# A cached-attention decode kernel: two heads to a K or V tile of 32 KB rows, three tiles instead of six, and the last rows of w4 in a tile of their own

## The chip, the cores and the metric

The kernel runs on one core of a Trainium2 chip. A core has TensorE (PE, with its weight loads shown apart as PEld), VectorE (DVE), ScalarE (ACT), GpSimd (POOL) and SyncE (SP), which here only issues transfers. Sixteen DMA engines move data from HBM into the core's SBUF, which has 128 partitions. The metric is the device time of one execution in microseconds. The kernel before takes 216.84 us (median of three runs, 216.29 to 216.96).

## The reference: what is computed

Four sequences (B = 4) each decode one token of width D = 576. The token is normalized, and two branches work on it.

```python
xn = _layernorm(x)
return x + _A_ref(xn, k_cache, v_cache, wq, wo) + _B_ref(xn, w1, w2, w3, w4)
```

The attention branch A has 32 query heads of width 128 on 16 key/value heads (`rep = 2` query heads share one). Only the last W = 2048 positions of the caches of 8192 count.

```python
q = (x @ wq).reshape(B, Sq, 32, Dh)
scores = einsum("bhqd,bhkd->bhqk", q, k[-W:]) * Dh ** -0.5
o = softmax(scores) @ v[-W:]
return o.reshape(B, Sq, 32 * Dh) @ wo
```

The MLP branch B ends in `x1 + gelu(layernorm(x1) @ w3) @ w4` with F = 4608 hidden values. Its first half adds to x a product of shifted pieces of h; as there is one position only, every shift brings in zeros, so x1 is x, and w1 and w2 are not loaded.

All data are bfloat16. K and V of the window are 67.1 MB, wq 4.7, w3 5.3, w4 5.3 and wo 4.7 MB: 87.2 MB in all, each read once.

## The kernel before, in words

**Tiles.** `load_kv` (L100) loads K or V of one key/value head in one DMA of 2 MB. A partition holds 64 consecutive positions of one batch entry, a row of 16,384 bytes: partition p belongs to batch p mod 4 and to the positions from 64 times p div 4 on. A pool of `NKV = 6` such tiles rotates. All transfers but one small one are issued by SP, in program order, and an issue waits until its tile is free.

**Order of the loads.** The list `order` (L515) is K of heads 0, 1, 2, then V of head h and K of head h + 3 in turn. A 1.15 MB piece of wo goes ahead of every fourth V. w3 follows V of head 2, the last 256 rows of w4 follow V of head 13, and the rest of w4 follows V of head 15 in six pieces. `flush_loads` (L523) issues from this list as long as the counter of free tiles allows; the counter grows at the end of each head's turn. wq, w3 and w4 share one buffer one after the other.

**The work of a head.** VectorE transposes a K tile in 32 x 32 blocks of 32-bit words, in two halves (`k_transpose`, L234). TensorE multiplies the result with the zero-padded queries `qz` (`k_scores`, L327): in four steps s, each of four matmuls of 512 columns. A zero-padded query block puts the eight scores rows of step s to rows 8s and on of a block of 32, so that all 128 partitions of one PSUM bank S are filled. `sm_max` masks the columns that belong to other batch entries and takes the row maximum, `sm_maxT` and `sm_neg` spread the maximum over the rows that share it, `sm_exp` (ScalarE) takes the exponential and its row sums, `sm_turn` transposes E into PT (VectorE), and `pv` (L406) multiplies PT with V in 16 matmuls, of which four run on four column groups of 32. `o_scale` divides by the softmax sums and adds the four slices (VectorE), `o_turn` and `o_sum` bring the result into head order. After each fourth head `o_spread`, `o_pick` and `o_proj` multiply by a piece of wo into the accumulator `acc`.

**Sums of the softmax.** The row sums of a head are split into three bfloat16 terms by GpSimd (`split`) and go through the next head's `sm_maxT` matmul; `sm_den` does it in a matmul of its own for the last head.

**Staging.** The order of all instructions is written out by hand (`manual_schedule`). In the turn of head t the K tile of t is transposed and scored, the softmax of t - 1 is done, PV of t - 2, and scaling of t - 3. The MLP's first product (`mlp_g`, in three slices) and its activation lie in the turn of head 7. Behind the loop come the last heads' softmax and PV, the product with the w4 tail, the last `o_proj`, and 68 matmuls with the rest of w4 (`mlp_out`, recorded as L194 like all products into `acc`). Then `acc` is copied and stored.

**The w4 tail.** The 256 last rows of w4 lie as two rows per partition, loaded in three DMAs of 100, 20 and 8 partitions.

Of the kernel before, what the change touches and what calls it, by code (L numbers as in the profile page):

```python
# [16 lines left out]
NKV = 6  # L17
# [5 lines left out]
def kernel(  # L23
# [29 lines left out]
    NJ = B * rep  # L53
    QD = 32
    NQD = P // QD
    NSL = 4
    SC = NC // NSL
    NI = 2
    CW = D // NI
    NW = SC * QD  # L60
# [20 lines left out]
    ptp = ctx.enter_context(tc.tile_pool(name="pt", bufs=2))  # L81
# [3 lines left out]
    ps_s = ctx.enter_context(tc.tile_pool(name="ps_s", bufs=2, space=PSUM))  # L85
    ps_o = ctx.enter_context(tc.tile_pool(name="ps_o", bufs=2, space=PSUM))
# [13 lines left out]
    def load_kv(kind, h):  # L100
        win = k_win if kind == "K" else v_win
        t = kvp.tile([P, NC, Dh], BF16, tag="kv", name=f"{kind.lower()}n")
        nc.sync.dma_start(out=t[:].rearrange("p c d -> p (c d)"),
                          in_=win[:, h].rearrange("b (p c) d -> p b (c d)", c=NC))
        kv_tiles[kind, h] = t
# [30 lines left out]
    SECTIONS = [(0, NFH), (P * NFH, NFH - 2), (F - 2 * P, 2)]  # L136
    SLOT = [0, NFH, NF - 2]
    W4_PIECES = [0, NFH, NFH + 5, NFH + 10, NFH + 14, NFH + 15, NFH + 16]
    TAIL_PARTS = [(0, 100), (100, 120), (120, P)]
    TAIL_AFTER = 13  # L140

    def w4_section(k):
        r0, n = SECTIONS[k]
        return B_w4[r0:r0 + P * n, :].rearrange("(p i) n -> p i n", i=n)

    def load_w4_tail():
        t = wp.tile([P, NF, D], BF16, tag="w", name="w4_sb")
        w_tiles["w4"] = t
        for lo, hi in TAIL_PARTS:
            nc.sync.dma_start(out=t[lo:hi, NF - 2:NF, :], in_=w4_section(2)[lo:hi])  # L150

    def load_w4():
        t = w_tiles["w4"]
        for lo, hi in zip(W4_PIECES, W4_PIECES[1:]):
            k = lo // NFH
            nc.sync.dma_start(out=t[:, lo:hi, :], in_=w4_section(k)[:, lo - SLOT[k]:hi - SLOT[k], :])

# [22 lines left out]
    gT = const.tile([P, NF, B], BF16, name="gT")  # L180
    op = const.tile([P, WOR, B], BF16, name="op")

    accs = [ps_acc.tile([P, CW], F32, name=f"acc{i}") for i in range(2)]
    for acc in accs:
        nc.vector.memset(acc[:], 0.0)

    def acc_of(i):
        return accs[i * 2 // NI][i * QD:i * QD + B, :]

# [44 lines left out]
    def k_transpose(h, half):  # L234
        c0 = half * 2 * SC
        src = kv_tiles["K", h][:].bitcast(I32)[:, c0:c0 + 2 * SC, :].rearrange("p c (ib i) -> p ib c i", i=QD)
        kt = ktp.tile([P, 2, 2 * SC, QD], I32, tag="kt")
        nc.vector.transpose(out=kt[:], in_=src)  # L238
        kts[h, half] = kt
# [3 lines left out]
    for kb in range(NQD):  # L243
# [3 lines left out]
    nc.vector.reduce_sum(out=oh4[:], in_=ident_f[:].rearrange("p (k b r) -> p b k r", b=B, r=rep), axis=AX.XY)  # L247
    mask = const.tile([P, QD], F32)
    nc.vector.tensor_scalar(out=mask[:].rearrange("p (q b) -> p q b", b=B),
                            in0=oh4[:].unsqueeze(1).to_broadcast([P, QD // B, B]), scalar1=-1.0, scalar2=BIG,  # L250
# [3 lines left out]
    NT = 3  # L254
    sel_j = const.tile([P, NJ], F32)
    nc.vector.reduce_sum(out=sel_j[:], in_=ident_f[:].rearrange("p (g j) -> p j g", j=NJ), axis=AX.X)
    sel_g = const.tile([P, NG], BF16)
    with nc.allow_low_precision("zeros and ones"):
        nc.vector.reduce_sum(out=sel_g[:], in_=ident_f[:].rearrange("p (g j) -> p g j", j=NJ), axis=AX.X)
# [5 lines left out]
    sel_s = const.tile([P, NSL], F32)  # L265
    nc.vector.reduce_sum(out=sel_s[:], in_=ident_f[:].rearrange("p (g s j) -> p s g j", s=NSL, j=NJ), axis=AX.XY)
# [27 lines left out]
    q_sb = bigp.tile([P, 2, NQD, Dh], BF16, tag="big", name="q_sb")  # L294
# [15 lines left out]
    for kb in range(NQD):  # L310
        rows = slice(kb * QD, (kb + 1) * QD)
        dst = qz[rows, ZP:].rearrange("p (x m) -> p x m", m=P)[:, :, kb * QD:kb * QD + NJ].rearrange("p x (b r) -> p x b r", r=rep)
        src = qs_ps[rows].rearrange("p h i r b -> p (h i) b r")
        if kb % 2:
            nc.scalar.activation(out=dst, in_=src, func=ACT.Copy)
        else:
            nc.vector.tensor_copy(out=dst, in_=src)
# [3 lines left out]
    E = {}  # L321
    PT = {}
    O_ps = {}
    O_sb = {}
    st = {}

    def k_scores(h, s):  # L327
        if s == 0:
            S_ps[h] = ps_s.tile([P, NW], F32, tag="S", name="S")
        half, c0 = s // 2, s % 2 * SC  # L330
        kt = kts[h, half][:].bitcast(BF16)
        if s % 2:
            kts.pop((h, half))
        for ie in range(4):
            ib, e = divmod(ie, 2)
            z0 = (h * 4 + ie) * P + ZP - s * NJ
            nc.tensor.matmul(out=S_ps[h][:], lhsT=qz[:, z0:z0 + P],  # L337
                             rhs=kt[:, ib, c0:c0 + SC, e:2 * QD:2].rearrange("p c k -> p (c k)"),
                             start=(s == 0 and ie == 0), stop=False, skip_group_check=True)

    def sm_max(h):
        mx = small.tile([P, 1], F32, tag="mx")
        S = S_ps[h][:].rearrange("p (c k) -> p c k", k=QD)
        nc.vector.tensor_tensor_reduce(out=S, in0=S, in1=mask[:].unsqueeze(1).to_broadcast([P, SC, QD]), scale=1.0,  # L344
                                       scalar=-3.0 * BIG, op0=ALU.add, op1=ALU.max, accum_out=mx[:])
        dm = dms.pop(h)
        nc.gpsimd.tensor_scalar(out=dm[:, 0:NG], in0=sel_g[:], scalar1=mx[:, 0:1], scalar2=scale,  # L347
                                op0=ALU.mult, op1=ALU.mult)
        st["dm", h] = dm

    def sm_maxT(h):
        n = NG + NT if h else NG
        mg = ps_m.tile([P, n], F32, tag="m", name="mg")
        nc.tensor.matmul(out=mg[:], lhsT=same_jb[:], rhs=st.pop(("dm", h))[:, 0:n], start=True, stop=True)
        st["mg", h] = mg

    def sm_neg(h):
        nm = small.tile([P, 1], F32, tag="nm")
        mg = st.pop(("mg", h))
        nc.vector.reduce_max(out=nm[:], in_=mg[:, 0:NG], axis=AX.X, negate=True)  # L360
        st["nm", h] = nm
        if h:
            dn = small.tile([P, 1], F32, tag="dn")
            nc.vector.reduce_sum(out=dn[:], in_=mg[:, NG:], axis=AX.X)  # L364
            sm_rec(h - 1, dn)

    def sm_exp(h):
        E[h] = ptp.tile([P, SC, QD], BF16, tag="e", name="E", bufs=1)
        rs = small.tile([P, 1], F32, tag="rs", name="rs")
        nc.scalar.activation(out=E[h][:].rearrange("p c k -> p (c k)"), in_=S_ps.pop(h)[:], func=ACT.Exp, scale=scale,  # L370
                             bias=st.pop(("nm", h))[:, 0:1],
                             accum_out=rs[:])
        st["rs"] = rs
        if h + 1 < Hkv:
            split(h + 1, rs)

    dms = {0: small.tile([P, NG + NT], BF16, tag="dm", name="dm")}

    def split(h, rs):
        dm = dms[h] = small.tile([P, NG + NT], BF16, tag="dm", name="dm")  # L380
# [25 lines left out]
    def pv(h, s):  # L406
# [7 lines left out]
        if s == NSL - 1:  # L414
            PT.pop(h)

# [242 lines left out]
```

## Time and profile before

| | us |
|---|---|
| median of three runs | 216.84 |
| the profiled execution, its own time | 216.09 |
| its span on the core | 214.3 |
| TensorE busy | 129.8 (61%) |
| VectorE busy | 134.6 (63%) |
| ScalarE busy | 24.1 (11%) |
| GpSimd busy | 31.0 (14%) |
| HBM read | 87.17 MB, 407 GB/s over the span |

A row of a group names line, engine and operation, what it writes and reads, the shapes and the count; behind the bar stand busy time, the mean duration of one in ns, and the engine's idle time just before them with what ended it. A row of the timeline starts with start and duration. In the view of stretches a row gives the length, then busy time and count of PE, PEld, DVE, ACT and POOL, then the granted clock of TensorE (1.00 is full), the busy share of the DMA engines and GB/s. The slices of the page cut the span into 40 equal parts of 5.36 us.

### The profile page before, as it was taken

What the parts mean: (1) busy time and instruction counts of PE and PEld (TensorE: products, weight loads), DVE (VectorE), ACT (ScalarE), POOL (GpSimd) and SP (SyncE); (2) the same over time, 40 slices, a digit from 0 to 9 for tenths busy, and PEclk for the clock granted to TensorE, in tenths of its full rate; (3) what the DMA queues carried; (4) which work ended last, traced back from release to release, by engine and by line L of the source; (5) the groups of instructions that cost most, each with busy time, mean ns of one, the idle gap of its engine ahead of it and who ended that gap; (6) DMA issues with size and microseconds to landing.
All of it is one profiled execution on the core that took longest, in us unless ns stands there. A gap on an engine that the chain in (4) does not pass through costs nothing.

```text
span 214.3 us, 2273 instructions
## 1 busy us (share of the span) xinstructions
PE 129.8 (61%) x824; PEld 46.8 (22%) x836; DVE 134.6 (63%) x247; ACT 24.1 (11%) x46; POOL 31.0 (14%) x134
## 2 busy tenths in 40 slices
PE   0048197676540076396984976676749557765593
PEld 0013032221210022121541322222212111322152
DVE  3620778898910296829459789597868764955500
ACT  6602201101000001100121010101101010011000
POOL 2250002122020002110014220202112120021000
PEclk9999769999995558967998899969997956996559
DMA  8999999999999999999999999999999999999960
GB/s 295 391 437 428 431 428 431 428 422 439 432 440 417 434 431 422 437 431 431 428 425 434 431 428 434 428 434 428 420 437 421 435 428 434 303 433 443 398 263 2
DMA packets 6815, 87.32 MB, mean 407 GB/s; under 512 B 776, under 2 KB 1044, under 8 KB 1812
## 3 DMA queue, kind: packets, MB, share of 16 engines
q1 hardware_dynamic: 6788, 87.17, 96.3%
q8 instruction: 6, 0.10, 0.2%
q14 instruction: 5, 0.04, 0.1%
q10 hardware_dynamic: 16, 0.01, 0.0%
HBM read 87.17 MB, written 0.00 MB: 407 GB/s over the span
## 4 chain that ended last, share of the span: by engine, by line
DMA 62%; DVE 13%; PE 10%; issue 1%; SPq 0%; DVEq 0%
DMA kn<-in_A_k_cache_dram 38%; DMA vn<-in_A_v_cache_dram 13%; DMA wo_sb<-in_A_wo_dram 11%; DVE kt L238 8%; PE acc L194 4%; PE g_ps L481 2%; DVE O_sb L422 2%; PE S L337 2%; PE O L412 1%; DVE S L344 1%; PE gT_ps L493 1%; DVE O_sb L420 1%; DVE op L459 0%; PE oT L428 0%; DVE mk L456 0%
## 5 line engine op out<-in xcount | busy, mean ns | idle before, releaser
L337 PE MATMUL S<-kt,qz 128*128 128x512 bf16 x244 | 77.3, 444 | 48.4 <-DVE kt L238 38.8
L238 DVE STREAM_TRANSPOSE kt<-kn 128x2048 int32<-128x2048 int32 x32 | 73.5, 2299 | 28.6 <-DMA kn<-in_A_k_cache_dram 27.0
L337 PEld LDWEIGHTS <-qz 128*128 128x128 bf16 x256 | 24.2, 108 | 87.6 <-DVE kt L238 39.2
L412 PE MATMUL O<-vn,PT 128*32 128x512 bf16 x256 | 24.9, 429 | 13.3 <-DMA vn<-in_A_v_cache_dram 12.9
L370 ACT ACTIVATE E<-S,nm 128x512 bf16<-128x512 f32 x16 | 11.0, 687 | 133.9 <-DVE dn L364 123.1
L422 DVE SCALAR_TENSOR_TENSOR O_sb<-O,rds,O_sb 128x128 f32<-128x128 f32 x48 | 16.8, 351 | 1.7
L347 POOL TENSOR_SCALAR dm<-sel_g,mx 128x16 bf16<-128x16 bf16 x16 | 4.4, 278 | 83.1 <-DVE mx L344 83.0
L392 DVE STREAM_TRANSPOSE PT<-E 128x512 bf16<-128x512 bf16 x16 | 11.3, 709 | 5.7 <-ACT E L370 5.7
L412 PEld LDWEIGHTS <-PT 128*32 128x32 bf16 x256 | 6.2, 97 | 36.1 <-issue 35.5
L403 POOL TENSOR_SCALAR rds<-sel_s,rd 128x4 f32<-128x4 f32 x16 | 4.8, 298 | 53.0 <-DVE rd L401 53.0
L344 DVE CUSTOM_DVE_ANT_1 S<-S,mask 128x512 f32<-128x512 f32 x16 | 10.8, 673 | 1.2 <-PE S L337 1.2
L437 DVE TENSOR_REDUCE on<-oT 128x8 bf16<-128x128 f32 x16 | 4.5, 280 | 5.6 <-PE oT L428 5.3
L420 DVE TENSOR_SCALAR O_sb<-O,rds 128x128 f32<-128x128 f32 x16 | 5.5, 345 | 3.0 <-PE O L412 3.0
L428 PE MATMUL oT<-ident_w,O_sb 128*128 128x128 f32 x16 | 6.0, 375 | 1.3 <-DVE O_sb L422 1.3
L226 PE MATMUL tp<-ident_bf,first 8*128 8x8 bf16 x4 | 0.3, 174 | 10.5 <-DVE first L218 10.5
L194 PE MATMUL acc<-w_sb,gT 128*4 128x288 bf16 x72 | 6.4, 349 | 0.0
L194 PE MATMUL acc<-wo_sb,op 128*4 128x288 bf16 x64 | 5.5, 324 | 1.0 <-DVE op L459 1.0
L384 POOL CAST dm<-rest 128x1 bf16<-128x1 f32 x30 | 5.6, 187 | 1.9
L625 DVE CAST fin<-acc 4x288 bf16<-4x288 f32 x1 | 0.4, 446 | 8.0 <-PE acc L194 8.0
L303 DVE COPY first<-qT_ps 128x64 bf16<-128x64 bf16 x2 | 0.3, 187 | 8.1 <-PE qT_ps L300 8.1
L481 PE MATMUL g_ps<-w_sb,ln2T 128*32 128x512 bf16 (+1 forms) x50 | 5.3, 474 | 0.0
L285 PE MATMUL q_ps<-wq_sb,xnT 128*32 128x512 bf16 x40 | 4.5, 631 | 0.0
(83 smaller groups left out, 82.0 us busy)
## 6 DMA issues: line engine op xcount, KB each, us to landing
kn<-in_A_k_cache_dram SPq DMA_DIRECT2D x16, 2048.0 KB, 25.4
vn<-in_A_v_cache_dram SPq DMA_DIRECT2D x16, 2048.0 KB, 26.7
wo_sb<-in_A_wo_dram SPq DMA_DIRECT2D x4, 1152.0 KB, 25.9
w_sb<-in_B_w_dram SPq DMA_DIRECT2D x1, 4608.0 KB, 31.7
wq_sb<-in_A_wq_dram SPq DMA_DIRECT2D x1, 4096.0 KB
w_sb<-in_B_w_dram SPq DMA_DIRECT2D x1, 2592.0 KB, 28.3
w_sb<-in_B_w_dram SPq DMA_DIRECT2D x2, 720.0 KB, 23.0
w_sb<-in_B_w_dram SPq DMA_DIRECT2D x2, 576.0 KB, 32.5
```

The lines of the kernel that those rows point to most:

```text
L194: nc.tensor.matmul(out=acc_of(i), lhsT=lhsT, rhs=rhs[:, i * CW:(i + 1) * CW], start=False, stop=False, skip_group_check=True)
L238: nc.vector.transpose(out=kt[:], in_=src)
L337: nc.tensor.matmul(out=S_ps[h][:], lhsT=qz[:, z0:z0 + P], rhs=kt[:, ib, c0:c0 + SC, e:2 * QD:2].rearrange("p c k -> p (c k)"), start=(s == ...
L344: nc.vector.tensor_tensor_reduce(out=S, in0=S, in1=mask[:].unsqueeze(1).to_broadcast([P, SC, QD]), scale=1.0, scalar=-3.0 * BIG, op0=ALU.a ...
L370: nc.scalar.activation(out=E[h][:].rearrange("p c k -> p (c k)"), in_=S_ps.pop(h)[:], func=ACT.Exp, scale=scale, bias=st.pop(("nm", h))[:, ...
L384: nc.gpsimd.tensor_copy(out=term, in_=left[:])
L392: nc.vector.transpose(out=PT[h][:], in_=E.pop(h)[:])
L412: nc.tensor.matmul(out=O_ps[h][g * QD:(g + 1) * QD], lhsT=PT[h][:, c, :], rhs=vn[:, :, c, :], start=(s == 0), stop=False, skip_group_check ...
L420: nc.vector.tensor_scalar(out=o[:], in0=O[:, 0, :], scalar1=w[:, 0:1], scalar2=None, op0=ALU.mult)
L422: nc.vector.scalar_tensor_tensor(out=o[:], in0=O[:, s, :], scalar=w[:, s:s + 1], in1=o[:], op0=ALU.mult, op1=ALU.add)
L428: nc.tensor.transpose(out=oT[:], in_=O_sb.pop(h)[:], identity=ident_f[:])
L481: nc.tensor.matmul(out=g_ps[g * QD:(g + 1) * QD], lhsT=ln2T[:, k, :], rhs=cols[:, :, i0:i0 + n], start=(j == 0), stop=False, skip_group_ch ...
```

## The change

A tile now holds two heads. `load_kv` takes a pair t and loads it in two DMAs, one per head: head 2t goes to the even partitions, head 2t + 1 to the odd ones. A row is 128 consecutive positions, 32,768 bytes, and a DMA has 64 of them. A tile is 4 MB, three of them rotate, in the same space. The last V tile is loaded in two halves of its rows, four DMAs.

The K tile is transposed in four quarters. Each step s of `k_scores` then has four matmuls for each of the two heads, on two PSUM banks, and reads every fourth bfloat16 of the transposed tile instead of every second. The exponentials of the two heads go into two tiles E0 and E1 that were cleared once, each into the columns of its own head; both are transposed to PT, so that one `pv` matmul has 64 weight columns and takes both heads. A pair has 32 of them on two column groups. There is one `o_scale`, `o_turn` and `o_sum` per pair. The softmax sums of every pair go through `sm_den`; `split` is gone.

The turn of pair t has the K of t, the softmax of t - 1, the first two thirds of PV of t - 1, the last third of PV of t - 2, and the scaling of t - 2. The counter of free tiles grows after steps 0 and 2 and loads are issued after every step. The MLP's three slices lie in the turns of pairs 3, 4 and 5. The load order is K of pairs 0 and 1, then V of t and K of t + 2 in turn; w3 follows V of pair 1.

The 256 last rows of w4 go into a kv tile of their own, behind the last V: 240 rows as three rows on 80 partitions, ten groups of eight, in one DMA, and 16 rows in a second. `mlp_g` and `mlp_turn` put the hidden values into that order with four more copies and a few more transposes, and `mlp_tail` multiplies them, between the two halves of PV of the last pair. PT has one buffer instead of two, S four banks instead of two, O one instead of two, and `acc` one bank instead of two.

```diff
-NKV = 6
+NKV = 3
...
+    NPR = Hkv // 2
+    NK = 2 * NC
+    QX = P // 4 // 2
...
-    ptp = ctx.enter_context(tc.tile_pool(name="pt", bufs=2))
+    ptp = ctx.enter_context(tc.tile_pool(name="pt", bufs=1))
...
-    ps_s = ctx.enter_context(tc.tile_pool(name="ps_s", bufs=2, space=PSUM))
-    ps_o = ctx.enter_context(tc.tile_pool(name="ps_o", bufs=2, space=PSUM))
+    ps_s = ctx.enter_context(tc.tile_pool(name="ps_s", bufs=4, space=PSUM))
+    ps_o = ctx.enter_context(tc.tile_pool(name="ps_o", bufs=1, space=PSUM))
...
-        t = kvp.tile([P, NC, Dh], BF16, tag="kv", name=f"{kind.lower()}n")
-        nc.sync.dma_start(out=t[:].rearrange("p c d -> p (c d)"),
-                          in_=win[:, h].rearrange("b (p c) d -> p b (c d)", c=NC))
+        kv = kvp.tile([P, NK, Dh], BF16, tag="kv", name=f"{kind.lower()}n")
+        n = NK // halves
+        for lo in range(0, NK, n):
+            for hh in range(2):
+                src = win[:, 2 * t + hh].rearrange("b (q c) d -> q b c d", c=NK)[:, :, lo:lo + n]
+                nc.sync.dma_start(out=kv[hh:P:2, lo:lo + n].rearrange("p c d -> p (c d)"),
+                                  in_=src.rearrange("q b c d -> q b (c d)"))
...
+    TG, TI, TU = 10, 8, 3
+    TA = TG * TI
+    TB = F - T0 - TA * TU
...
+        nc.sync.dma_start(out=t[0:TA, 0:TU * D],
+                          in_=B_w4[T0:T0 + TA * TU, :].rearrange("(i g u) n -> g i (u n)", g=TG, u=TU))
+        nc.sync.dma_start(out=t[0:TB, TU * D:(TU + 1) * D], in_=B_w4[F - TB:F, :])
...
-    accs = [ps_acc.tile([P, CW], F32, name=f"acc{i}") for i in range(2)]
+    acc = ps_acc.tile([P, CW], F32, name="acc")
...
+    def k_transpose(t, s):
+        src = kv_tiles["K", t][:].bitcast(I32).rearrange("p (c s) (ib i) -> p s ib c i", s=NSL, i=QD)[:, s]
+        kt = ktp.tile([P, 2, SC, QD], I32, tag="kt")
+        nc.vector.transpose(out=kt[:], in_=src)
...
+        for hh in range(2):
+            for ie in range(4):
+                ib, e = divmod(ie, 2)
+                z0 = ((2 * t + hh) * 4 + ie) * P + ZP - s * NJ
+                nc.tensor.matmul(out=S_ps[t, hh][:], lhsT=qz[:, z0:z0 + P], rhs=kt[:, ib, 2 * hh + e::4],
+                                 start=(s == 0 and ie == 0), stop=False, skip_group_check=True)
...
+        for hh in range(2):
+            nc.scalar.activation(out=E[hh][:, :, hh:QD:2], in_=S_ps.pop((t, hh))[:].rearrange("p (c k) -> p c k", k=QX),
+                                 func=ACT.Exp, scale=scale, bias=nm[:, hh:hh + 1], accum_out=rs[:, hh:hh + 1])
...
+        PT = ptp.tile([P, SC, 2, QD], BF16, tag="pt", name="PT")
+        for hh in range(2):
+            nc.vector.transpose(out=PT[:, :, hh, :], in_=E[hh][:])
...
+        for c in range(lo, hi):
+            g = c % 2
+            nc.tensor.matmul(out=O[g * 2 * QD:(g + 1) * 2 * QD], lhsT=PT[:, c].rearrange("p k m -> p (k m)"), rhs=vn[:, c],
+                             start=(c < 2), stop=False, skip_group_check=True)
...
+    order = [("K", 0), ("K", 1)]
+    for t in range(NPR):
+        order.append(("V", t))
+        if t + 2 < NPR:
+            order.append(("K", t + 2))
+    W3_AFTER = ("V", 1)
...
+            load_kv(kind, t, 2 if (kind, t) == order[-1] else 1)
...
+        if pos["n"] == len(order) and pos["free"] > 0:
             pos["n"] += 1
+            load_w4_tail()
             load_w4()
...
+    G_AT = [3, 4, 5]
     k_transpose(0, 0)
+    for t in range(NPR):
+        a, b, c = t - 1, t - 2, t - 3
         for s in range(NSL):
+            if s == 0:
+                if a >= 0:
+                    sm_max(a)
+                k_transpose(t, 1)
+                k_scores(t, 0)
+                if b >= 0:
+                    pv(b, PV_CUTS[2], PV_CUTS[3])
+                    pos["free"] += 1
+                if c >= 0:
+                    o_pick(c)
+            elif s == 1:
+                if a >= 0:
+                    sm_maxT(a)
+                k_scores(t, 1)
+                if a >= 0:
+                    sm_neg(a)
+                    sm_exp(a)
+                k_transpose(t, 2)
+                if b >= 0:
+                    o_scale(b)
+                if c >= 0:
+                    o_proj(c)
+            elif s == 2:
+                if a >= 0:
+                    sm_turn(a)
+                    sm_den(a)
+                k_transpose(t, 3)
+                k_scores(t, 2)
+                if a >= 0:
+                    sm_rec(a)
+                if b >= 0:
+                    o_turn(b)
+                if a >= 0:
+                    pv(a, PV_CUTS[0], PV_CUTS[1])
+                if t in G_AT:
+                    mlp_g(G_AT.index(t))
+                pos["free"] += 1
+            else:
+                if b >= 0:
+                    o_sum(b)
+                if t + 1 < NPR:
+                    k_transpose(t + 1, 0)
+                k_scores(t, 3)
+                if b >= 0:
+                    o_spread(b)
+                if a >= 0:
+                    pv(a, PV_CUTS[1], PV_CUTS[2])
...
+            flush_loads()
...
+    pv(a, 0, SC // 2)
+    mlp_tail()
+    pv(a, SC // 2, SC)
```

## The prediction

> **What bounds the kernel now.** I read the page's slices, its DMA queues and its chain first, then the groups and the K tile's own view, then two stretches and the timeline.
>
> ```profile
> span 214.3 us, 2273 instructions
> PEclk9999769999995558967998899969997956996559
> DMA  8999999999999999999999999999999999999960
> GB/s 295 391 437 428 431 428 431 428 422 439 432 440 417 434 431 422 437 431 431 428 425 434 431 428 434 428 434 428 420 437 421 435 428 434 303 433 443 398 263 2
> q1 hardware_dynamic: 6788, 87.17, 96.3%
> DMA 62%; DVE 13%; PE 10%; issue 1%; SPq 0%; DVEq 0%
> ```
>
> The DMA engines are full from the second slice to the 37th, at about 430 GB/s, with one dip to 303 in slice 35. The chain agrees: 62% DMA. So the span is: 1.8 us until packets flow, about 207 us of packets, and what follows the last V tile. The packet records of the trace give the unit prices: 4102 packets of 16,384 B with a median of 611 ns, and 128 of 32,768 B (wq) with a median of 1213 ns.
>
> ```profile
> L238 DVE STREAM_TRANSPOSE kt<-kn 128x2048 int32<-128x2048 int32 x32 | 73.5, 2299 | 28.6 <-DMA kn<-in_A_k_cache_dram 27.0
> L392 DVE STREAM_TRANSPOSE PT<-E 128x512 bf16<-128x512 bf16 x16 | 11.3, 709 | 5.7 <-ACT E L370 5.7
> DMA to landing us min/median/max: 17.2/25.4/37.6
> 120.53 1.08 PE L337 MATMUL S<-kt,qz 128*128 128x512 bf16 x4
> 120.20 0.40 PE L412 MATMUL O<-vn,PT 128*32 128x512 bf16 x4
> ```
>
> Two groups of the page, the K tile's view and two rows of the timeline. Compute follows the loads: VectorE waits 27.0 us for K tiles. The third line is that of the K tiles: from issue to landing 25.4 us, five tile times of 4.88 us (2.10 MB at 430 GB/s), so a tile is given back early and about 20 us of work stand queued ahead of it. One score matmul costs 0.27 us, and four PV matmuls on four column groups of 32 run beside each other in 0.27 to 0.4.
>
> ```profile
> 183.00:187.50 4.50, 2.91 (x28) 1.26 (x25) 4.33 (x11) 0.19 (x1) 0.14 (x1) 1.00 1.00 287
> 203.00:211.00 8.00, 7.83 (x84) 4.48 (x84) 0.14 (x1) 0.11 (x1) 0.00 (x0) 0.67 0.51 204
> 197.15 1.90 PE L412 MATMUL O<-vn,PT 128*32 128x512 bf16 x16 [2.42 <-DMA vn<-in_A_v_cache_dram]
> 202.94 2.08 PE L194 MATMUL acc<-wo_sb,op 128*4 128x288 bf16 x16 [0.97 <-DVE op L459]
> 204.81 6.02 PE L194 MATMUL acc<-w_sb,gT 128*4 128x288 bf16 x68
> ```
>
> The first row (busy time per engine, then clock, DMA share, GB/s) is the dip: the w4 tail goes to 100, 20 and 8 partitions, and while it is in flight 68 of V's own 16,384 B packets take 640 to 1182 ns. Excess over nominal, tail included: 24 us summed, 1.5 us per engine. The end: V of head 15 lands at 197.15, PV and scaling follow, 84 matmuls end at 210.86. The last w4 packets end near 208.6, so the chain of compute ends last.
>
> **The change, part by part.** The sum is made against the profiled execution: span 214.3, own time 216.09; the median 216.84 lies 0.75 above that.
>
> *Rows of 32 KB.* A pair of 16 KB packets costs 1222 ns, one of 32 KB 1213: 9 ns. Up to the last V tile each engine moves 15 tiles x 8 such packets: 120 x 9 = 1.1 us earlier. The count of DMAs stays (two per tile of two heads). Whether 64 rows on every other partition run at 1213 ns is not shown by any row; every K, V and weight load of before uses 128 adjacent partitions. Lower bound: the 1213 of wq, no loss. Upper: the 1182 seen for a 16 KB packet (1.93 times) on all of them, 8 tiles x 2 x 8 x 1213 ns x 0.93 = +144 us. I take no loss, since wq is the same packet size on the same queue, and keep the other end as a rival.
>
> *The tail row of w4* moves from before V of head 14 to behind V of the last pair. Its 295 KB (0.69 us at 430) and the 1.5 us of slowness leave the stretch ahead of the last V: 2.2 us. It is again a load to fewer than 128 partitions, so I let the slowness happen later, beside w4, where 2 us of slack stood. A tail without slowness would give nothing more, as w4 does not end last.
>
> *Three tiles instead of six halves.* The same bytes, given back in pieces of 4.19 MB (9.75 us). A tile must be given back within two tile times of its landing, 19.5 us, less 0.4 from last packet to semaphore and 1.1 from issue to first packet (first wq issue 0.72, first packet 1.8): 18.0. K of pair t is held by VectorE: four transposes 9.2, two maxima 1.35 (0.67 each), nm 0.15 and a wait of 0.3, one o_scale 1.47, two PT transposes at twice the columns, 1.25 each by L392 = 2.5: 15.0 us, 15.8 where o_pick (0.85) falls in. V is held until K of two pairs on has landed (9.75), a K transpose 2.3, eight score matmuls 2.15, eleven PV matmuls: 15.9. These now sit on two groups of 64 columns, so two run beside each other: 5.5 x 0.27 = 1.5. Margin 2 us at full clock. At half clock the eight and the eleven double: +3.6, 1.6 late. With ten or so reissues past the third pair, three in ten at the half clock: none to 5 us of starved queue. The wo loads (1.18 MB, 2.7 us) before every other V add margin to half of them, and a single throttled quantum of 3.4 us slips PE by 1.7 at most: I take 0.5. Behind each waiting K issue on SP stands only the next V issue.
>
> *Work.* Per pair VectorE saves one o_scale (1.47) and one on (0.28), and pays 1.1 for PT: near 126 us instead of 134.6, hidden under the 27 us of K waits. If that cover is gone, it is the hold time above. PV on PE takes twice as long (24.9 to near 45 us busy), hidden while scores (8.6 us per pair) and PV (4.3) stay under 19.5 us. The added ScalarE copies of the third MLP slice and GpSimd's second product hide under ScalarE at 11% and GpSimd at 14%. At the start K of pair 0 lands at 1.8 + 8.91 MB / 0.43 = 22.5, before the first transpose at 23.95: nothing. One acc bank instead of two: nothing.
>
> *The end.* V of the last pair lands at 197.15 - 1.1 - 2.2 = 193.9, so K of pair 7 (V 4.19, V 4.19, wo 1.18 MB before that: 22.2 us) at 171.7, with the stall 172.2. From there: VectorE 15.0 to the last K transpose, eight scores 2.15, both maxima 1.35, o_pick 0.85; PE meanwhile has 22 PV matmuls, 3.0, and the maximum's transpose at +20.8. Then nm, o_scale of pair 6 in front, exp beside it, two PT transposes 2.5: PV of pair 7 starts at +25, 3 us after its V landed. So halving that V brings nothing here, and waiting for the tail behind V costs nothing (it lands near 195.4). PV 2.15, eight tail matmuls 0.7, PV 2.15, then o_scale to op as before, 3.7: +33.7. The 84 matmuls cost 7.9 at before's clock (0.50, then 1.0 from 208.2). At full clock, by the last 39 of them (68 ns each), they cost 5.7; I take 6.8. End: 172.2 + 33.7 + 6.8 = 212.7 against 210.86: +1.8. So 216.84 + 1.8 = **218.6 us**.
>
> **A rule weighed.** The row first: during the w4 tail, on 100 partitions, the rate fell from 428 to 287 GB/s. [...]
>
> **The rivals.**
> 1. *Faster.* The granted clock stays at 1.0 through the last 40 us, since PE has less idle time than the 2.4 us before 197.15; no queue starves, and the tail's slowness is gone. Then 84 matmuls cost 5.7 and the stall 0: 1.8 - 1.1 - 0.5 = +0.2. With exp and o_scale overlapping 1.5 us better than my count, -1.3 or more: about 215.3. It decides from a start of PV of pair 7 before +23.5.
> 2. *Same.* Only part of that: within 0.3% (0.65 us, about what this kernel's runs can tell from no change).
> 3. *Half-partition loads collide.* For: the dip. Against: V's packets, to 128 partitions, slowed as much as the tail's, so it may be no matter of partitions. With the mean slowed packet of the dip (894 of 611 ns): 155 x 0.46 = +72, near 289 us.
> 4. *PE becomes the bound.* Score columns are now read at steps of 8 B instead of 4. If that doubles 0.27 us, scores and PV take 21.5 us of 19.5 per pair, plus 1.5 for the rest: 8 x 3.5 = +28, near 245. No row shows a step of 8 B, nothing speaks for it.
> 5. *The row gain does not come:* then 1.1 more, 219.7, inside the forecast.
>
> **How the numbers follow.** Forecast with 5: 0.41 (own range 217.5 to 226, the top with 5 us of starving and half clock in PV, +4). Faster 0.23, same 0.12, collision 0.20, PE 0.04. Faster 0.23, same 0.12, slower 0.65. The low end 214.3 is the faster case with one us more. The high end leaves out most of the collision: 236, which a mild one (packets 12% longer, +19) still reaches. Outside are about 0.18 above and 0.03 below.
>
> **What would show it.** Right: K packets at 1213 ns and 430 GB/s in the slices; issue to landing of K down from 25.4 to 12 to 15 us; short DMA gaps only where the clock is halved; VectorE near 126 us; PV of the last pair released by PT, not by V; acc ending near 212.7. Wrong: GB/s near 250 to 300 in K and V slices (rival 3); score matmuls over 0.4 us at full clock (rival 4); many empty DMA slices (the hold times mis-sized); acc ending before 210.2 (rival 1).

## The result, and the profile after

The changed kernel takes 377.59 us (median of six runs, 373.26 to 381.14), the kernel before in the same job 216.14 (six runs, 215.93 to 216.96). The ratio is 1.736, with an interval of 1.724 to 1.747: slower by 161 us, where 218.6 had been forecast with a range up to 236. Some executions of any of these kernels are one to three per cent longer than the others; the medians count them, the ratios leave them out.

The page of the changed kernel, slices, DMA queue and chain:

```profile
span 371.5 us, 2143 instructions
PEclk9975897858587855586776987695857985776958
DMA  8999999999999998999999999999999999999990
GB/s 340 335 215 201 208 285 208 201 222 222 222 213 322 362 221 188 270 208 212 219 215 222 217 205 248 217 215 226 228 226 243 233 220 236 227 213 254 256 397 29
q1 hardware_dynamic: 4866, 87.17, 97.5%
DMA 72%; PE 14%; DVE 8%; another core or an unknown queue 3%; SPq 1%; issue 0%; ACT 0%; DVEq 0%
```

The DMA engines are as full as before (97.5% of the span), the bytes are the same 87.17 MB, yet slices of K and V move mostly 200 to 245 GB/s where before moved 430. A slice is now 9.3 us. The two slices at 322 and 362 are those in which w3 is loaded (slices 13 and 14), and the one at 397 belongs to w4: those loads kept their form and most of their rate (w3's large packets have a mean of 1514 ns, 1366 before). So no queue ran empty; each packet of K and V takes longer. The packet records of the trace say so directly: the 1920 packets of 32,768 B of K and V have a median of 2386 ns (mean 2395), against 1213 for wq's of the same size before; the 256 of 16,384 B (the last V) a median of 1052 against 611.

Two groups of the page:

```profile
L247 DVE STREAM_TRANSPOSE kt<-kn 128x2048 int32<-128x2048 int32 x32 | 73.4, 2297 | 181.6 <-DMA kn<-in_A_k_cache_dram 178.6
L342 PE MATMUL S<-kt,qz 128*128 128x512 bf16 x256 | 120.0, 629 | 110.5 <-DVE kt L247 110.5
```

and the last line of the K tile's own view:

```profile
DMA to landing us min/median/max: 18.6/33.3/50.0
```

From issue to landing K takes 33.3 us (25.4 before). VectorE waits 178.6 us for K tiles (27.0 before); TensorE waits 110.5 us for VectorE, which passes the same wait on. The score matmul's mean has gone from 444 to 629 ns, of which more below.

Packet durations summed over the records and divided by 16 engines make 362.4 us, before 206.4: +156.0, and the span grew by 371.5 - 214.3 = 157.2. Nearly the whole loss is in that sum: 1920 x (2395 - 1213) ns / 16 = 142 us for the K and V rows, 7 us for the halves of the last V, 6 us for wo, whose packets ran beside them (mean 540 ns instead of 349), and 2.9 us for w3 and w4. That is 158, 2 too many: before's own 16 KB packets had a mean of 617 ns, so that two of them took 1234 and not 1213.

### The profile page after: what moved, and what is told of

Its sections match the earlier page's. It is cut to its first block, busy times and chain, and to the rows that moved or that the text cites. A ratio compares the mean times of both kernels' runs of the same rounds, so it can differ in the third digit from the quotient of the medians.

```text
span 371.5 us, 2143 instructions
## 1 busy us (share of the span) xinstructions
PE 190.5 (51%) x842; PEld 62.2 (17%) x842; DVE 126.9 (34%) x178; ACT 26.6 (7%) x52; POOL 12.9 (3%) x52
## 3 DMA queue, kind: packets, MB, share of 16 engines
q1 hardware_dynamic: 4866, 87.17, 97.5%
HBM read 87.17 MB, written 0.00 MB: 235 GB/s over the span
## 4 chain that ended last, share of the span: by engine, by line
DMA 72%; PE 14%; DVE 8%; another core or an unknown queue 3%; SPq 1%; issue 0%; ACT 0%; DVEq 0%
DMA kn<-in_A_k_cache_dram 66%; PE S L342 8%; DMA w_tail<-in_B_w_dram 6%; DVE kt L247 6%; PE O L405 4%; PE acc L204 2%; SPq L110 1%; DVE PT L378 1%; DVE O_sb L415 1%; PE mg L358 0%; SPq L165 0%; DVE O_sb L413 0%; DVE on L430 0%; PE oT L421 0%
## 5 line engine op out<-in xcount | busy, mean ns | idle before, releaser
L342 PE MATMUL S<-kt,qz 128*128 128x512 bf16 x256 | 120.0, 629 | 110.5 <-DVE kt L247 110.5
L247 DVE STREAM_TRANSPOSE kt<-kn 128x2048 int32<-128x2048 int32 x32 | 73.4, 2297 | 181.6 <-DMA kn<-in_A_k_cache_dram 178.6
L405 PE MATMUL O<-vn,PT 128*64 128x512 bf16 x256 | 43.3, 475 | 45.6 <-DMA vn<-in_A_v_cache_dram 44.2
L342 PEld LDWEIGHTS <-qz 128*128 128x128 bf16 x256 | 28.4, 117 | 183.6 <-issue 180.6
L405 PEld LDWEIGHTS <-PT 128*64 128x64 bf16 x256 | 16.6, 130 | 72.4 <-issue 63.0
L378 DVE STREAM_TRANSPOSE PT<-E 128x1024 bf16<-128x1024 bf16 x16 | 18.9, 1216 | 0.0
L415 DVE SCALAR_TENSOR_TENSOR O_sb<-O,rds,O_sb 128x128 f32<-128x128 f32 x24 | 8.4, 351 | 0.9
L413 DVE TENSOR_SCALAR O_sb<-O,rds 128x128 f32<-128x128 f32 x8 | 2.5, 318 | 7.5 <-PE O L405 7.5
L204 PEld LDWEIGHTS <-gT 128*4 128x4 bf16 (+2 forms) x76 | 3.9, 98 | 4.8 <-issue 2.7
L383 PEld LDWEIGHTS dn<-rs,same_j 128*128 128x128 f32 x16 | 3.0, 200 | 4.7 <-issue 3.4
L184 ACT ACTIVATE qz<-zero 128x4108 f32<-128x4108 f32 x1 | 3.6, 3609 | 0.0
## 6 DMA issues: line engine op xcount, KB each, us to landing
kn<-in_A_k_cache_dram SPq DMA_DIRECT2D x16, 2048.0 KB, 33.3
```

Of the source, the lines that this page charges most:

```text
L184: nc.scalar.activation(out=flat, in_=zero[:].bitcast(F32).to_broadcast(list(flat.shape)), func=ACT.Copy)
L204: nc.tensor.matmul(out=acc_of(i), lhsT=lhsT, rhs=rhs[:, i * CW:(i + 1) * CW], start=False, stop=False, skip_group_check=True)
L342: nc.tensor.matmul(out=S_ps[t, hh][:], lhsT=qz[:, z0:z0 + P], rhs=kt[:, ib, 2 * hh + e::4], start=(s == 0 and ie == 0), stop=False, skip_g ...
L378: nc.vector.transpose(out=PT[:, :, hh, :], in_=E[hh][:])
L405: nc.tensor.matmul(out=O[g * 2 * QD:(g + 1) * 2 * QD], lhsT=PT[:, c].rearrange("p k m -> p (k m)"), rhs=vn[:, c], start=(c < 2), stop=Fals ...
L415: nc.vector.scalar_tensor_tensor(out=o[:], in0=O[:, s, :], scalar=w[:, s:s + 1], in1=o[:], op0=ALU.mult, op1=ALU.add)
```

## The experiments

Two loads of 64 rows replaced one of 128, rows doubled, partitions went to every other one, tiles became three: each can be undone or done alone. In the first four expectations theory A is that loads to every other partition collide on their way into SBUF, rival B that the rows of 32 KB and how they are read cost the time, and rival C that DMAs of 64 rows are slow wherever they go. The kernel before was timed in each job; its medians there were 215.73 (the first four runs), 216.24 (the next four), 215.38 (three) and 215.69 (the last).

**Every other partition, in the kernel before.** Same bytes to the same places.

```diff
-        nc.sync.dma_start(out=t[:].rearrange("p c d -> p (c d)"),
-                          in_=win[:, h].rearrange("b (p c) d -> p b (c d)", c=NC))
+        for k in range(2):
+            nc.sync.dma_start(out=t[k:P:2].rearrange("p c d -> p (c d)"),
+                              in_=win[k:B:2, h].rearrange("b (p c) d -> p b (c d)", c=NC))
```

> The kernel before with one edit: each K or V tile of one head is loaded in two DMAs of 64 rows of 16 KB, one for the even partitions and one for the odd ones, instead of one DMA of 128 rows. Everything else stays. [...] Rival B (the rows of 32 KB and how they are read cost the time): rows stay at 16 KB, so 216 to 218 us. [...]

Measured: 214.76 us, ratio 0.9945 (0.9915 to 0.9975), packets at 611 ns. Theory A as worded fell: 64 rows on every other partition are not slow in themselves. The page's rate and its queue:

```profile
GB/s 289 415 412 430 418 435 426 421 427 438 430 440 411 440 440 410 442 436 430 424 421 433 440 415 440 440 421 418 430 433 433 424 433 433 331 409 425 417 251 4
q1 hardware_dynamic: 7300, 87.17, 96.3%
```

**Two DMAs by columns, in the kernel before** (128 partitions each, rows of 8 KB).

> The kernel before with each K or V load cut in two DMAs by columns: 128 partitions x 8 KB each, so twice the DMAs and packets, and the same partitions as before. Theories A, B and C: no collapse; two packets of 8 KB for one of 16 KB cost some 9 ns more each, 256 per engine, so 217 to 220 us. If the number of DMAs per tile were the cause, this would slow down like the changed kernel.

Measured: 216.28 us, ratio 1.0026 (0.9994 to 1.0058). That is below the 217 to 220 us expected. Two packets of 8 KB do take 618 ns instead of 611, and the packets' sum per engine grows from 206.4 to 208.4 us, but in the time twice the DMAs and half the packet cost 0.6% at most. So the number of DMAs is not the cause.

**One DMA of 128 rows of 32 KB, in the changed kernel.** It takes 4096 positions of one head instead of 2048 of two, so the sums it computes are of other data; bytes, tiles and all instructions but the loads stay.

```diff
+        full = (A_k_cache if kind == "K" else A_v_cache)[:, 2 * t, Sk - 2 * W:Sk, :]
...
-            for hh in range(2):
-                src = win[:, 2 * t + hh].rearrange("b (q c) d -> q b c d", c=NK)[:, :, lo:lo + n]
-                nc.sync.dma_start(out=kv[hh:P:2, lo:lo + n].rearrange("p c d -> p (c d)"),
-                                  in_=src.rearrange("q b c d -> q b (c d)"))
+            src = full.rearrange("b (q c) d -> q b c d", c=NK)[:, :, lo:lo + n]
+            nc.sync.dma_start(out=kv[:, lo:lo + n].rearrange("p c d -> p (c d)"),
+                              in_=src.rearrange("q b c d -> q b (c d)"))
```

> The changed kernel with one DMA of 128 rows of 32 KB per tile: the rows come from 4096 positions of one head in place of 2048 of two (so K and V are other data, and the output is not the reference's); bytes, tile, waits and all compute stay. Theory A: packets at 1213 ns, 430 GB/s, and the rest of the forecast comes to the test: 214 to 221 us, K issue to landing 12 to 15 us. Rival B: rows of 32 KB over four batch entries are still read in step, so it stays at 350 to 378. Rival C: as A.

Measured: 222.7 us, ratio 1.031 (1.024 to 1.038), just above the 214 to 221 expected, packets back at 1213 ns. 155 of the 161 us hang on how the tile is loaded; 7 are something else.

**Engines put out of step, in the changed kernel.** Two added loads of rows of 8 KB, ahead of K, are counted in twelve groups and in four. My assumption, which no trace shows, was that a load goes to as many engines as it has groups: four engines would get sixteen packets, eight engines eight and four engines none, and these three sets would start K two packets of 32 KB (eight of 8 KB) apart.

```diff
+    late = ktp.tile([P, 2, SC, QD], I32, tag="kt", name="late")[:].rearrange("p a c k -> p (a c k)").bitcast(BF16)
+    nc.sync.dma_start(out=late[0:96], in_=A_wq[0:96].rearrange("(i g) n -> g i n", g=12))
+    nc.sync.dma_start(out=late[96:P], in_=A_wq[96:P].rearrange("(i g) n -> g i n", g=4))
```

> The changed kernel with two added loads ahead of the first K tile, into a buffer that is not needed yet: 96 rows of 8 KB in twelve groups, then 32 rows in four groups, 1.05 MB in all (2.5 us of DMA). [...] Rivals B and C: no change but the added 2.5 to 5 us, 378 to 383.

Measured: 368.54 us, ratio 1.706; below the range of B and C, and much too slow for a cure by theory A. But the slices show a partial success:

```profile
GB/s 346 336 296 442 243 265 384 424 310 301 289 283 222 239 223 130 216 190 230 226 135 223 233 233 220 226 190 217 226 194 219 188 243 218 207 223 267 349 76 3
```

In most of the first twelve slices of 9.1 us the rate is well above 220. By stretches of 30 us from 10 us after the first packet, the K and V packets' means are 1498, 1479, 1662, 2063, 2255 and 2422 ns. Behind the added loads the same packets to the same partitions ran for 60 us at means below 1500 ns, 2395 without those loads; then they slowed down again. A slow row or a slow partition would not care for the time at which an engine starts; a collision between engines would.

So I worded it anew, theory M: what counts is which partitions one DMA engine writes while others write theirs. A DMA of K has its source counted as positions by batches. In the kernel before the outer count is 32, in the changed one 16. With 64 rows for sixteen engines that would leave each engine one block of positions with its four batches, four rows that lie over eight neighbouring partitions; this is my assumption, and no trace shows which rows an engine takes. The run on every other partition had 32 by 2. Three runs for that.

**The count alone, in the kernel before.** Every other partition again, 16 KB rows, but 16 by 4 (so other positions land on a partition).

```diff
+        src = win[:, h].rearrange("b (p c) d -> p b (c d)", c=NC)
+        for k in range(2):
+            nc.sync.dma_start(out=t[k:P:2].rearrange("p c d -> p (c d)"),
+                              in_=src[k * PB // 2:(k + 1) * PB // 2])
```

> The kernel before with each K and V tile loaded by two DMAs of 64 rows of 16 KB to every other partition, as in the run with even and odd partitions, but with the source's rows counted as 16 positions by 4 batches instead of 32 by 2 (other positions land on other partitions, so the output is not the reference's; bytes, rows, packets and partitions are the same). Theory M (what slows a load is which partitions one DMA engine writes: with 16 outermost each engine writes four rows that spread over eight neighbouring partitions, and another engine writes its partitions at the same time): 16,384 B packets near twice 611 ns, 1150 to 1250, time 350 to 378 us. Rival R (rows of 32 KB are what is slow on 64-row loads) and rival S (no load of this kind is slow in this kernel): packets 611 ns, 214 to 217 us.

Measured: 357.32 us (353.42 and 361.22). Packets of 16,384 B: median 1141 ns. Its slices and its queue on the page:

```profile
GB/s 351 310 226 222 277 221 224 224 229 223 402 317 230 222 238 249 222 222 228 230 226 228 230 251 229 228 232 232 230 233 230 217 261 233 233 235 242 262 386 32
q1 hardware_dynamic: 7300, 87.17, 97.8%
```

The same picture as the changed kernel, with six tiles, 16 KB rows and nothing else of the change. Beside 214.76 us for 32 by 2, with the same partitions, length of rows, bytes and number of DMAs, the count of the source, and with it which of its rows one DMA reads, is the cause.

**The count alone, in the changed kernel.** Its two DMAs per tile, 64 rows of 32 KB on every other partition, counted as 32 by 2 (4096 positions of one head, two batches per DMA).

```diff
-                src = win[:, 2 * t + hh].rearrange("b (q c) d -> q b c d", c=NK)[:, :, lo:lo + n]
+                src = full[hh:B:2].rearrange("b (q c) d -> q b c d", c=NK)[:, :, lo:lo + n]
```

> The changed kernel with its two DMAs per tile, 64 rows of 32 KB to every other partition, left as they are in number, size and partitions; only the source is counted as 32 positions by 2 batches of one head instead of 16 by 4 (it reads other data, so the output is not the reference's). Theory M: packets back at 1213 ns, time 220 to 226 us, as with one DMA of 128 rows (222.7). Rival R (64 rows of 32 KB on every other partition are slow however they are counted): packets near 2350 ns, 368 to 380 us.

Measured: 225.23 us, ratio 1.042 (1.035 to 1.050), 32 KB packets at 1213 ns, and the page's rate is back:

```profile
GB/s 283 470 376 470 440 371 440 461 429 417 454 409 429 408 465 392 477 393 452 440 411 285 470 396 473 376 470 426 417 288 440 426 423 410 432 294 408 322 2 2
```

Number, size and partitions of the DMAs are those of the changed kernel; the other count of the source, and with it other rows read, undoes the slowness.

**Two adjacent halves, 16 by 4, in the kernel before.** Partitions 0 to 63 and 64 to 127.

```diff
+        src = win[:, h].rearrange("b (p c) d -> p b (c d)", c=NC)
+        for k in range(2):
+            nc.sync.dma_start(out=t[k * P // 2:(k + 1) * P // 2].rearrange("p c d -> p (c d)"),
+                              in_=src[k * PB // 2:(k + 1) * PB // 2])
```

> The kernel before with each K and V tile loaded by two DMAs of 64 rows of 16 KB, to partitions 0 to 63 and 64 to 127, source counted as 16 by 4. [...] Rival (every other partition is what is slow): 214 to 217 us.

Measured: 375.19 us (one run), packets at a median of 1225 ns. No row is on every other partition here, and the four rows that theory M assumes for an engine would be neighbours; still each packet takes twice as long as the 611 ns of the kernel before. So if partitions are what the engines share, it is not between neighbours alone. These two DMAs read the same source rows as the two of the slow run on every other partition, though. That the engines meet in reading these rows from HBM, wherever they are written, is a rival that this run does not exclude.

**The step of the score matmuls, in the changed kernel with one DMA of 128 rows.** The 512 columns are taken from one half of the transposed tile at a step of 4 bytes, not from all of it at 8; the scores are then of other positions.

```diff
-                nc.tensor.matmul(out=S_ps[t, hh][:], lhsT=qz[:, z0:z0 + P], rhs=kt[:, ib, 2 * hh + e::4],
+                nc.tensor.matmul(out=S_ps[t, hh][:], lhsT=qz[:, z0:z0 + P], rhs=kt[:, ib, 2 * NW * hh + e:2 * NW * (hh + 1):2],
```

> The changed kernel with one DMA of 128 rows per tile (222.7 us), and the score matmuls reading their 512 columns at a step of 4 bytes instead of 8 (the columns of one half of the tile instead of one head's, so the output is not the reference's; same count and size). Theory P (what is left of the loss, 222.7 against 215.7, is TensorE: a score matmul takes 0.47 us instead of 0.265, so K and V tiles come free late): score matmuls 0.265 us at full clock, TensorE busy 182 down to 125 to 135 us, time 216 to 219 us. Rival H (three tiles of 4 MB starve the queue whatever TensorE takes, through VectorE's 15 us on each K tile): matmuls quicker, time 221 to 224 us.

Measured: four runs, 218.67, 219.63, 222.85 and 223.46 (median 221.24), too far apart for a ratio. The lower two, near theory P's range, lie below all runs with the step of 8 (222.1 to 223.3, and one of 228.5); so a gain of about 3 us is likely, but rests on these two. Eight score matmuls, in the timeline of the changed kernel and of this one:

```profile
106.08 3.78 PE L342 MATMUL S<-kt,qz 128*128 128x512 bf16 x8
```

```profile
67.51 1.97 PE L342 MATMUL S<-kt,qz 128*128 128x512 bf16 x8
```

0.47 us each at a step of 8 bytes, 0.25 at 4, both at a granted clock of 1.00. What that does to the queue is seen in the page's slices, first of the run with 32 by 2 (step 8, profiled at 225.05 us), then of this one (219.63 us). The two differ in their loads as well, two DMAs to a tile there and one here:

```profile
PE   0048199999899900699999999999999899987593
DMA  7989989999999999999997999899979999999800
```

```profile
PE   0048189667197700396759596959595369596492
DMA  7999999999999999998999999999999999999920
```

With slow matmuls TensorE has stretches without a gap, and the queue has dents in slices 22 and 30. By the packet records, up to the end of the last load and less the packets' own sum per engine, the engines were idle for 3.8 us there, 2.2 us with the quick matmuls, and 0.4 us in the kernel before. From the end of the last load to the store of the result it is another 8.7, 5.5 and 4.1 us. So with slow matmuls 3.4 us more than before are an empty queue, and 4.6 us more are work left over behind the loads; with quick ones it is 1.8 and 1.4. How the dent at 118 us comes about, in the timeline of the first of the two:

```profile
113.37 3.77 PE L343 MATMUL S<-kt,qz 128*128 128x512 bf16 x8
117.07 1.48 PE L406 MATMUL O<-vn,PT 128*64 128x512 bf16 x11
118.58 1.86 SPq L111 DMA_DIRECT2D kn<-in_A_k_cache_dram  x2
```

The K load waits for the V tile that the last third of PV gives back, and that third stands behind eight score matmuls. By the packet records at most eight of the sixteen engines are busy from 118.9 to 120.6 us, at the least two, until the packets of that load arrive.

**The same slow step in the kernel before.** Is it the matmuls, or the matmuls on three large tiles?

```diff
-                             rhs=kt[:, ib, c0:c0 + SC, e:2 * QD:2].rearrange("p c k -> p (c k)"),
+                             rhs=kt[:, ib, :, e:2 * QD:4].rearrange("p c k -> p (c k)"),
```

> The kernel before with the score matmuls reading their 512 columns at a step of 8 bytes instead of 4, from both halves of the transposed tile's columns (so the output is not the reference's; same count and size). By the changed kernel's runs a score matmul should then take 0.47 us instead of 0.265 at full clock, TensorE's busy time rise from 130 to about 175 us. Theory C (the slow matmuls cost time only because three large tiles leave two tile times to give one back; with six small ones the queue stays full): 215 to 217.5 us, no empty slices. Rival (slow matmuls cost what they take wherever they are, 3 us and more, as between 222.7 or 225.2 and 221.2 us on the three tiles): 218.5 to 224 us.

Measured: 215.19 us, ratio 0.9978 (0.9955 to 1.0001). The page's busy times, and a group of four in the timeline:

```profile
PE 170.7 (80%) x836; PEld 47.2 (22%) x836; DVE 135.9 (64%) x247; ACT 24.1 (11%) x46; POOL 31.3 (15%) x134
```

```profile
107.15 1.96 PE L337 MATMUL S<-kt,qz 128*128 128x512 bf16 x4
```

Four take 1.96 us instead of 1.06, TensorE works 40 us more, and nothing is lost: up to the end of the last load the DMA engines are idle for 0.4 us, as in the kernel before. With six tiles the load that waits has others queued ahead of it: K takes a median of 22.6 us from issue to landing there, 14.3 in the run with 32 by 2 on three tiles.

**The w4 tail in one DMA, in the kernel before.** By theory M the dip in slice 35 should be the same thing in small.

```diff
-    TAIL_PARTS = [(0, 100), (100, 120), (120, P)]
+    TAIL_PARTS = [(0, P)]
```

> The kernel before with the tail row of w4 loaded by one DMA of 128 partitions instead of three of 100, 20 and 8. The prediction held that the three cost 1.5 us ahead of the last V tile, since V's packets beside them took 640 to 1182 ns. If the cause is which partitions their engines write (theory M again, on a small load), the dip in slice 35 goes and the last V lands up to 1.5 us earlier: 214.2 to 215.5 us beside a before of 215.7 to 216.2. If the dip is due to something else (the small packets of 2304 B, the place in the queue), or the last V is not what the end waits for: within 0.3% of before.

Measured: 212.81 us, ratio 0.9865 (0.9831 to 0.9900), a larger gain than expected, and the fastest of the simple edits. The page's slices, and two rows of the timeline:

```profile
GB/s 300 397 431 425 435 422 441 410 441 430 480 405 402 435 435 409 444 428 435 435 419 438 431 427 433 428 431 428 430 435 428 428 429 425 432 434 433 411 367 16
```

```profile
195.20 1.90 PE L412 MATMUL O<-vn,PT 128*32 128x512 bf16 x16 [1.59 <-DMA vn<-in_A_v_cache_dram]
202.85 5.39 PE L194 MATMUL acc<-w_sb,gT 128*4 128x288 bf16 x68
```

The dip to 303 is gone. The tail's 128 packets take 93 ns each instead of a mean of 132, and the mean of all 16 KB packets falls from 617 to 613. Summed per engine the packets make 204.8 instead of 206.4 us, PV of the last head starts at 195.20 instead of 197.15, and the last products end at 208.24 instead of 210.83. Of these 2.6 us, 0.6 come from the products themselves (5.39 instead of 6.02 us, at a granted clock of 0.80 instead of 0.71); the expectation had left that out. The run does not separate the tail's partitions from its count of rows; that three DMAs became one should not matter, by the run with two DMAs by columns.

**Both edits, and the first one again.**

> The kernel before with both edits: K and V by two DMAs on odd and even partitions (214.76 beside 215.73 us before), and the tail row of w4 in one DMA of 128 partitions. If both gains are real and apart, 213.3 to 214.3 us, the fastest of all; if the first gain is only that the tail collides less, 214.3 to 215 us, no better than one alone.

> The same kernel as the run with even and odd partitions, a second time. If its gain of 0.55% (interval 0.25 to 0.85%) was real, the ratio is 0.992 to 0.998 again; if it was the chip's or the runs' scatter, 0.998 to 1.003.

Measured: both edits 212.62 us, ratio 0.9862 (0.9828 to 0.9897), below both expectations and not to be told from the tail alone; every other partition a second time 215.31 us, ratio 0.9983 (0.9961 to 1.0005). Its first gain of 0.55% was mostly scatter. The version to keep is the kernel before with the tail in one DMA: it beats both kernels of this case.

## Why the prediction was wrong

**The step that failed** is "Rows of 32 KB": "I take no loss, since wq is the same packet size on the same queue". wq's packets go to 128 adjacent partitions; the size was the same, the count of the source's rows was not. In its place the runs showed K and V packets with a mean of 2395 ns instead of 1213, 142 us by themselves. It came with the count 16 by 4 and went with 32 by 2, in either kernel (packets of 1141 against 611 ns, and 2386 against 1213). The measured +156 us lies just over the upper end that the same paragraph had worked out from the slowest packet of the dip, +144. The rival of colliding loads was named, but had a chance of 0.20 and a price of +72, from the mean packet of the dip (its 155 us are the 8 x 2 x 8 packets of 1213 ns per engine). That mean probably counts packets that met the tail for a part of their time only, while nearly all of K and V ran slow throughout.

**The argument against the rival was wrong too.** V's own packets to 128 partitions had been slowed in the dip, and I read that as "no matter of partitions". The run with the tail in one DMA took both away at once, with the same bytes at the same place in the queue: it was a matter of the tail's partitions and count, and V's packets suffered for it.

**The w4 tail.** The slowness was put at 1.5 us per engine; undone, it gave 1.6 us in the packets' sum. The size held, and so did the guess that the load to fewer than 128 partitions is behind it. In the changed kernel the tail is still on 80 and 16 partitions (3456 B packets at a mean of 262 ns, 188 to 206 in the three runs of it without slow K and V).

**Score columns at 8 bytes** (rival 4): "nothing speaks for it". It did double: four more matmuls cost 0.91 us at a step of 4 bytes (1.97 for eight, 1.06 for four) and 1.81 at 8 (3.77 and 1.96). The price of +28 us was too high. It counted 21.5 us for scores and PV of a pair and 1.5 for the rest; the 32 score matmuls take 15.1 us and PV 4.6 (36.8 us for eight pairs, with one DMA of 128 rows), which just about fills the 19.5 us of the pair's loads. TensorE came near to being the bound all the same, as the chain of the run with 32 by 2 shows:

```profile
PE 48%; DMA 33%; DVE 12%; issue 2%; POOL 1%; SPq 1%; ACT 1%; ACTq 0%; DVEq 0%; POOLq 0%
```

**Three tiles.** The stall was put at 0.5 us, the range at 0 to 5. Without the slow packets the queue is empty for 3.8 us, 3.4 more than before; with quick matmuls 2.2, 1.8 more. Both lie inside the range and above the value taken. The hold time of V was worked out with score matmuls of 0.27 us (its terms add up to 15.7 us, not 15.9), so a part of this came by the slow score matmuls. K's issue to landing, forecast at 12 to 15 us, has a median of 14.3 (32 by 2) and 15.5 us (quick matmuls).

**Work and end.** VectorE is busy 126.9 us (forecast 126), but the savings that the prediction lists, about 0.65 us for each of eight pairs, come to 129 only, so the nearness is partly luck. PV on TensorE is busy 43.3 us (45), and 35 to 37 in the runs without slow packets. The end can be read from the run with neither slow packets nor slow matmuls:

```profile
173.91 2.31 DVE L247 STREAM_TRANSPOSE kt<-kn 128x2048 int32<-128x2048 int32 x1 [6.13 <-DMA kn<-in_A_k_cache_dram]
198.74 1.92 PE L405 MATMUL O<-vn,PT 128*64 128x512 bf16 x16 [1.41 <-DVE rd L388]
208.11 5.77 PE L204 MATMUL acc<-w_sb,gT 128*4 128x288 bf16 x68
```

The last K is taken up at 173.9 (forecast 172.2), PV of the last pair starts 24.8 us later (25) and is released by VectorE, not by V, and the products end at 213.88 (212.7). So halving the last V brought nothing there, as said. Of the 1.1 us that longer rows were to save, the packets of K and V show 0.8 in this run and 0.6 in the one with 32 by 2 (157.0 and 157.2 us per engine, 157.8 before). In the changed kernel itself the tail's product did wait 1.82 us for its load, which the prediction had excluded; that load too stood behind slow packets.

**What stays open.** No trace here shows which engine writes which partition, so the assignment behind theory M is an assumption, tried on three counts only. Nor is it shown that the engines meet, and where: every slow load of K or V counted its source 16 by 4, and every fast one 32 by 2 or 32 by 4, so a collision in reading HBM is not told from one on the way into SBUF. Why the engines of the out-of-step run slowed down again after some 90 us was not tried. With quick matmuls 1.8 us of empty queue and 1.4 us behind the loads are left against before; which waits cause them was not tried. I found no way to write 2048 positions of two heads in rows of 32 KB with an outer count of 32, so the changed kernel's own data were not run with fast packets.

## What to carry to other kernels

When a load's shape changes, compare the access pattern and not only the packet size: here 16 KB packets of loads counted 16 by 4 had medians of 1141 and 1225 ns, of loads counted 32 by 2 or 32 by 4 of 611, so look at the outermost count, and at the rows and partitions of each DMA. DMA engines as full as before (97.5% and 96.3% of the span) at half the GB/s (200 to 245 where 430 had been), with packets of the same size twice as long (2386 ns against 1213), pointed to that; a short dip beside a load to fewer partitions (287 GB/s) may be the same thing in small and is worth an experiment on its own, which here gave 1.35%. A slow instruction cost nothing while six tiles rotated (215.19 us, before 215.69). With three it came with an empty queue (3.8 us, 2.2 with the quick one) and work left over behind the loads (8.7 us against 5.5), so its price is worked out with the tiles' hold times.

## What the runs showed of the hardware

- Two ways to load a tile in two DMAs of 64 rows of 16 KB, to the same partitions, differed by 1.87 in the packet (median 611 and 1141 ns), through the count of their source, 32 by 2 or 16 by 4, and with it the rows that one DMA reads.
- The slowness depends on time: behind two added loads of rows of 8 KB, meant to put the engines out of step, the 32 KB packets of K and V had means of 1480 to 1500 ns for 60 us and then slid back to 2420; without those loads their mean is 2395.
- One more matmul of 512 bfloat16 columns cost 0.45 us where it reads every fourth element (8 bytes; eight took 3.77 us, four 1.96), and 0.23 where it reads every second (1.97 and 1.06 us).
